# A kernel of attention and two MLPs: the second turn of the first MLP's results added in DRAM by the storing DMA

## The chip, the cores and the metric

The kernel runs on one core of a Trainium2 chip. The metric is the device time of one execution in microseconds; the median of several executions is compared. In the texts PE is TensorE (the matmul engine), PEld its loading of weights, DVE VectorE, ACT ScalarE, POOL GpSimd, and SP SyncE, which here issues nearly all DMAs. Each engine takes its own instructions in order; an instruction that reads what another engine writes waits for a semaphore.

## The reference, cut to what matters

```python
def reference(q, k, v, moe, moe2):                 # q, k, v: 4 x 8 heads x 576 x 64
    scores = (q @ k.transpose(0, 1, 3, 2)) / 8.0
    scores = where((rel >= 0) & (rel < 128), scores - slopes * abs(rel), -1e9)
    attn = softmax(scores) @ v
    x = attn.transpose(0, 2, 1, 3).reshape(2304, 512)
    h = x @ moe.w_in                               # 512 -> 2048
    x = (maximum(h, 0) + moe.alpha * minimum(h, 0)) @ moe.w_out
    h = maximum(maximum(x @ moe2.w1, x @ moe2.w2), x @ moe2.w3)   # 512 -> 768
    return h @ moe2.w_out                          # 2304 x 512
```

All of it is in fp32. `rel` is the distance of a key behind its query, so each token attends to itself and the 127 tokens before it.

## The kernel before, in words

The kernel has three stages that overlap: the attention, the first MLP and the second MLP. A matmul of fp32 numbers is done as three matmuls on rounded parts: each operand is split into a high part (an ACT cast, L521) and the rest (a subtraction on DVE or POOL, L523). Some weights are first put into another form of words by a chain of small steps on ACT, DVE and POOL (L501 to L514); these are the many `v<-v` and `wt<-wt` steps of a trace.

Attention: scores (L872), a pass over them on DVE (L903), exponentials on ACT (L909, L914), a scaling on POOL (L921), transposes by a matmul with the identity (L931), a copy of the transposed block out of PSUM on ACT (L939, into `w_d` early and into `pt` later), the values (L951, early L968 and L975), and copies of the result out of PSUM (L983 for the late groups, L998 and L1000 for the others).

First MLP: the 2304 tokens lie in nine blocks of 256, in five groups, `GROUPS = ((0, 1), (2, 3), (4,), (5, 6), (7, 8))`. For groups 0 to 2 a hidden step computes 128 hidden units (12 matmuls: L1034, L1035, L1036), DVE applies the activation (L1040, L1043), ACT and DVE split the result into `g` (L1013, L1014), and 12 products (L1062) add to the group's four PSUM banks `xb`. A step is of 512 columns for groups 0 and 1, and of 256 for group 2 and the first steps of group 0. `JOBS` sets the sequence: group 0 with hidden units 0 to 8 (its first turn), group 1 with all 16, group 0 with units 9 to 15 (its second turn), group 2. Groups 3 and 4 are computed by `pair_mlp`, with block products in fewer multiplications (L679, L713); group 4 in two turns, by halves of the hidden units.

Where a group has two turns (0 and 4), each turn's results are copied out of PSUM (L1077, or L727 in `drain`) and stored in a DRAM tile of its own, `x2d0_0` and `x2d0_1`, `x2d4_0` and `x2d4_1`. `sum_of_turns(k)` (L566) loads both in eight pieces of 128 KB, adds them on POOL (L563) and stores the sum in a third tile, from which the second MLP reads (`tokens`, L1087). The second MLP (`second_mlp`, L1082) has products L1225, L1250 and L1350 and starts when the pair MLP is done.

What sets the order: every piece of work is an `Op` of a `Plan` with its engine and dependencies, and the order in which all of them are issued, on all engines, is written out in a packed table, `ORDER`. `Plan.issue` (L137) goes through it, models the start of each op, and where the model sees a gap on PE between 12 and 130 us it puts matmuls that compute nothing into the next free bank (L461, `FILL_ONE` 0.215 us each in the model). L455 and L623 are single matmuls of the same kind that the table places. Pools of buffers set further waits: `o` and `ve` have two buffers, `wt` and `g` three, `hb` and `sb` two PSUM banks each, `xb` four banks that one group holds at a time.

## Time and profile before

| | us |
|---|---|
| median of 3 executions | 775.29 (775.09 to 775.59) |
| the profiled execution | 775.46 |
| its span, first to last instruction | 773.6 |
| PE busy | 758.2 (98%) |
| DVE busy | 577.5 (75%) |
| ACT busy | 447.3 (58%) |
| POOL busy | 283.9 (37%) |
| DMA queue of SP | 67.8% of 16 engines |

All durations that follow come from the profiled execution. Its granted PE clock is 1.00 in all stretches shown, of 2.4 GHz. A row of the timeline gives the start, the duration, the engine, the line, the operation and its tiles, and in square brackets how long the engine had been idle before and what released it. A busy time can hold overlapping instructions, since matmuls are pipelined: what one costs is read from start to start.

### The profile page before, as it was taken

To read this page: it belongs to the slowest core of one execution; us is meant where nothing else is said; L and a number is where in the kernel's file an instruction comes from. 1 tells how busy PE (TensorE), PEld (TensorE's weight loads), DVE (VectorE), ACT (ScalarE), POOL (GpSimd) and SP (SyncE) were. 2 spreads that over 40 slices of the span, in tenths; PEclk is the share of its full clock that TensorE was granted. 3 is DMA by queue.
4 is the path that set the end of the run, shared out by engine and by line. 5 is a ranking of instruction groups with operands and counts; after the bars stand their busy time and mean duration, and the time that the engine had idled before them with its cause. 6 is when DMAs were issued, how large, how long until landed. Compare 5 with 4: busy or idle time off the path is not lost.

```text
span 773.6 us, 17304 instructions
## 1 busy us (share of the span) xinstructions
PE 758.2 (98%) x6018; PEld 665.4 (86%) x6022; DVE 577.5 (75%) x1457; ACT 447.3 (58%) x1235; POOL 283.9 (37%) x385
## 2 busy tenths in 40 slices
...
GB/s 306 289 233 254 167 167 250 171 198 191 208 193 177 162 249 190 92 215 182 262 230 233 374 141 223 272 312 271 340 261 244 319 361 367 179 300 240 182 2 83
DMA packets 93096, 175.75 MB, mean 227 GB/s; under 512 B 11088, under 2 KB 53712, under 8 KB 93008
## 3 DMA queue, kind: packets, MB, share of 16 engines
q1 hardware_dynamic: 92544, 174.11, 67.8%
...
## 4 chain that ended last, share of the span: by engine, by line
PE 93%; ACT 3%; DMA 1%; DVE 1%; issue 0%; ACTq 0%; SPq 0%; DVEq 0%
PE xb L1062 15%; PE sb L1225 13%; PE hb L1225 13%; PE xb L713 6%; PE xb L1350 5%; PE hb L1034 5%; PE sb L679 5%; PE hb L679 5%; PE hb L1035 5%; PE hb L1036 5%; PE sb L951 3%; PE hb L713 3%; PE sb L713 3%; PE sb L931 3%; PE sb L872 2%; PE xb L1250 2%
## 5 line engine op out<-in xcount | busy, mean ns | idle before, releaser
L1062 PE MATMUL xb<-g,w_a 128*128 128x512 f32 (+1 forms) x624 | 125.3, 347 | 0.6 <-DVE z L903 0.6
L1062 PEld LDWEIGHTS xb<-g,w_a 128*128 128x128 f32 x624 | 97.5, 189 | 18.6 <-issue 5.8
L921 POOL TENSOR_SCALAR p<-p,z 128x192 f32<-128x192 f32 x144 | 74.1, 530 | 67.5 <-DVE z L917 63.0
L1034 PE MATMUL hb<-x_a,w_a 128*128 128x512 f32 (+1 forms) x208 | 73.5, 353 | 0.6 <-DVE x_a L1000 0.6
L909 ACT ACTIVATE p<-p,z 128x192 f32<-128x192 f32 x144 | 64.5, 452 | 12.2 <-DVE z L903 11.3
L1035 PE MATMUL hb<-x_a,w_a 128*128 128x512 f32 (+1 forms) x208 | 70.9, 341 | 0.0
L1036 PE MATMUL hb<-x_a,w_a 128*128 128x512 f32 (+1 forms) x208 | 70.8, 340 | 0.0
L514 POOL TENSOR_TENSOR v<-v,p 128x192 int32<-128x192 int32 (+1 forms) x72 | 41.6, 580 | 62.7 <-DVE v L511 21.8
L1225 PE MATMUL sb<-w_e,w_a 128*128 128x384 f32 x306 | 59.5, 335 | 0.0
L514 POOL TENSOR_TENSOR wt<-wt,w_b 128x512 int32<-128x512 int32 x32 | 42.9, 1344 | 30.5 <-issue 10.4
L1225 PEld LDWEIGHTS sb<-w_e,w_a 128*128 128x128 f32 x306 | 53.5, 188 | 0.2
L1013 ACT CAST g<-hb 128x512 fp32r<-128x512 f32 (+1 forms) x52 | 25.3, 486 | 42.0 <-DVE hb L1043 40.2
L523 DVE TENSOR_TENSOR w_a<-wt,w_a 128x512 fp32r<-128x512 f32 (+1 forms) x60 | 43.5, 728 | 7.4 <-ACT w_a L521 5.3
L521 ACT CAST w_a<-wt 128x512 fp32r<-128x512 f32 (+1 forms) x78 | 42.9, 563 | 9.5 <-DVE wt L563 4.0
L713 PE MATMUL xb<-g,w_a 128*128 128x512 f32 x192 | 46.8, 389 | 0.0
L1225 PE MATMUL hb<-w_e,w_a 128*128 128x384 f32 x234 | 46.4, 334 | 0.0
L1034 PEld LDWEIGHTS hb<-x_a,w_a 128*128 128x128 f32 x208 | 39.4, 189 | 7.2 <-issue 1.7
L1225 PE MATMUL hb<-w_e,x_a 128*128 128x384 f32 x234 | 45.2, 335 | 0.0
L1040 DVE TENSOR_SCALAR t<-hb,alpha_sb 128x512 f32<-128x512 f32 (+1 forms) x52 | 32.3, 621 | 15.9 <-PE hb L1036 15.4
L903 DVE CUSTOM_DVE_ANT_0 p<-sb,rel 128x192 f32<-128x192 f32 x112 | 35.3, 352 | 11.0 <-PE sb L872 4.9
L1036 PEld LDWEIGHTS hb<-x_a,w_a 128*128 128x128 f32 x208 | 39.4, 189 | 4.5
L1035 PEld LDWEIGHTS hb<-x_a,w_a 128*128 128x128 f32 x208 | 39.5, 190 | 3.7
...
## 6 DMA issues: line engine op xcount, KB each, us to landing
...
```

The source lines that it names most:

```text
L514: add("pool", 0.08 + n / 430, due - 5, lambda: nc.gpsimd.tensor_tensor(out=wt().bitcast(I32), in0=wt().bitcast(I32), in1=words(0), op=ALU. ...
L521: add("act", 0.05 + n / 1100, due, lambda: nc.scalar.copy(w()[:, 0, :n], of()), r=[of], w=[w])
L523: add("pool" if pool_lo else "dve", 0.08 + n / 430 if pool_lo else 0.07 + n / 960, due + 1, lambda: eng.tensor_tensor(out=w()[:, 1, :n], i ...
L679: nc.tensor.matmul(to(), w()[:, a, ws], xs[k]()[:, b], start=(first and at_m == 0), stop=(last and at_m == 5), skip_group_check=True)
L713: nc.tensor.matmul(bs[m](), W_out[f]()[:, a, cols], g[f]()[:, b], start=(opens and f == fs[0] and not a and not b), stop=(closes and f == ...
L909: exps.append(add("act", 0.45, due - 10 + a, lambda i=i, n=n, p=p: nc.scalar.activation(out=part_of_p(p, n), in_=part_of_p(p, n), func=AF. ...
L921: z.readers.append(add("pool", 0.4, at_a + 0.2, lambda i=i, n=n, p=p: nc.gpsimd.tensor_scalar(out=part_of_p(p, n), in0=part_of_p(p, n), sc ...
L1034: nc.tensor.matmul(to, wi()[:, 0, ws], x[:, 0, cols], start=(kk == 0), stop=False)
L1035: nc.tensor.matmul(to, wi()[:, 1, ws], x[:, 0, cols], start=False, stop=False)
L1036: nc.tensor.matmul(to, wi()[:, 0, ws], x[:, 1, cols], start=False, stop=(kk == KD - 1))
L1062: nc.tensor.matmul(to, wo()[:, a, ms], g()[:, b, :n], start=(opens and not a and not b), stop=(closes and ends), skip_group_check=apart)
L1225: nc.tensor.matmul(to()[:, :TILE], Qs[q]()[:, a, ws], x[:, b], start=(first and n == 0), stop=(last and n == 5), skip_group_check=True)
```

## The change

`sum_of_turns` goes, and with it 32 loads, 16 adds on POOL and 16 stores. Each group has one DRAM tile, `x2d0` to `x2d4`. A new helper, `stored`, issues the stores: those of a first or only turn as before from SP; those of the second turn of groups 0 and 4 from POOL, with `accum_op=ALU.add`, so that the DMA adds its data to what lies in DRAM. There are four such DMAs for each of the two groups, 256 KB each. In the plan they are still counted as SP's, at twice the cost of a plain store. `tokens` reads the group's one tile.

The table `ORDER` is another one altogether (one line of each stands below), and the model puts 29 fillers (L461 before, L458 after) instead of 17.

```diff
@@ -250,116 +250,113 @@
 ORDER = (
-    'c-'
...
+    'c-jrq0|FR2768B(JE?8kwr$(C-TvCPZQHhO+qSzqcNh!|5<p_0Pzn-3Nhl5-'
...
@@ -563,19 +560,13 @@
         add(eng, 0.08 + n / 430 if eng == "pool" else 0.07 + n / 960, due, lambda: e.tensor_tensor(
             out=to(), in0=one(), in1=two(), op=op), r=[one, two, *inplace], w=[to], port=True)
 
-    def sum_of_turns(k, due):
-
-        x2_d[k, 2] = dram.tile([P, KD, 2 * N], F32, name=f"x2d{k}_2")
-        x2_b[k, 2] = Buf(None, None, None)
-        for i in range(2 * KD):
-            kk, cols = i // 2, slice(i % 2 * N, (i % 2 + 1) * N)
-            u, w = (ve_r.new().part(lambda t: t.rearrange("p a b d -> p (a b d)")) for _ in range(2))
-            for one, turn in ((u, 0), (w, 1)):
-                add("sp", 0.5, due + 8 * i, lambda one=one, turn=turn, kk=kk, cols=cols: nc.sync.dma_start(
-                    out=one(), in_=x2_d[k, turn][:, kk, cols]), r=[x2_b[k, turn]], w=[one])
-            add_two("pool", N, due + 8 * i + 4, u, u, w, ALU.add)
-            add("sp", 0.5, due + 8 * i + 5, lambda u=u, kk=kk, cols=cols: nc.sync.dma_start(
-                out=x2_d[k, 2][:, kk, cols], in_=u()), r=[u], w=[x2_b[k, 2]])
+    def stored(due, cost, o, key, view, again, of=lambda t: t):
+
+        b = x2_b[key]
+        if again:
+            add("sp", 2 * cost, due, lambda: nc.gpsimd.dma_start(out=view(x2_d[key]), in_=of(o()), accum_op=ALU.add), r=[o, b], w=[b])
+        else:
+            add("sp", cost, due, lambda: nc.sync.dma_start(out=view(x2_d[key]), in_=of(o())), r=[o], w=[b])
 
     def words_ahead(due, until):
 
@@ -722,8 +713,7 @@
                 o = o_r.new() if m == 3 or key != (4, 1) else g_r.new().part(lambda t: t[:, 0].bitcast(F32))
                 copy, eng = ((nc.scalar.copy, "act"), (nc.vector.tensor_copy, "dve"))[m % 2]
                 add(eng, 0.62, due + six * m, lambda m=m, o=o, copy=copy: copy(o(), bs[m]()), r=[bs[m]], w=[o])
-                add("sp", 1.0, due + six * m + 1, lambda m=m, o=o: nc.sync.dma_start(
-                    out=x2_d[key][:, m, :], in_=o()), r=[o], w=[x2_b[key]])
+                stored(due + six * m + 1, 1.0, o, key[0], lambda t, m=m: t[:, m, :], key == (4, 1))
 
         whole = x_b.new()
         oA, now, s, E = [whole.part(lambda t, m=m: t[m]) for m in range(KD)], begin, 0, {}
@@ -800,7 +790,7 @@
             drain(oB, (4, half), now + six)
             now += 4 * six
             if not half:
-                stores = x2_b[4, 0].writers[-1:]
+                stores = x2_b[4].writers[-1:]
                 for f in range(8):
                     fetch_weights("in", f, IN_AT[f], now - 20 + 2 * f, stores if f > 3 else ())
                 for f in range(8):
@@ -1002,8 +992,7 @@
                 in1=part_of(x, 0, n).bitcast(F32), op=ALU.subtract), r=[psv[n]], w=[x], after=[hi])
 
 
-    x2_d = {(k, turn): dram.tile([P, KD, len(cs) * N], F32, name=f"x2d{k}_{turn}")
-            for k, cs in enumerate(GROUPS) for turn in range(2 if k in (0, 4) else 1)}
+    x2_d = {k: dram.tile([P, KD, len(cs) * N], F32, name=f"x2d{k}") for k, cs in enumerate(GROUPS)}
     x2_b = {key: Buf(None, None, None) for key in x2_d}
     st = {"turn": 0}
 
@@ -1075,8 +1064,7 @@
                 o = o_r.new()
             copy, eng = ((nc.scalar.copy, "act"), (nc.vector.tensor_copy, "dve"))[m % 2]
             add(eng, 0.12 + n / 1000, due, lambda m=m, o=o, copy=copy: copy(o()[:, :n], x2()[m][:, :n]), r=[x2], w=[o])
-            add("sp", n / 512, due, lambda m=m, o=o, turn=turn: nc.sync.dma_start(
-                out=x2_d[k, turn][:, m, :], in_=o()[:, :n]), r=[o], w=[x2_b[k, turn]])
+            stored(due, n / 512, o, k, lambda t, m=m: t[:, m, :], k == 0 and not turn, lambda t: t[:, :n])
 
 
     def second_mlp(begin):
@@ -1091,8 +1079,7 @@
                 g0, g1 = cs[0] * N, (cs[-1] + 1) * N
                 a, b = max(lo, g0), min(lo + TILE, g1)
                 if a < b:
-                    key = (k, 2 if k in (0, 4) else 0)
-                    yield x2_b[key], x2_d[key][:, kk, a - g0:b - g0], slice(out_at, out_at + b - a)
+                    yield x2_b[k], x2_d[k][:, kk, a - g0:b - g0], slice(out_at, out_at + b - a)
                     out_at += b - a
 
         def right_of(p, due):
@@ -1613,10 +1600,8 @@
             todo.append((i, hidden_of(i)))
             later(LATER)
     later(0)
-    sum_of_turns(0, at[-1])
     words_ahead(at[-1] + 60, at[-1] + 150)
     begin = pair_mlp(at[-1])
-    sum_of_turns(4, begin + 10)
     second_mlp(begin)
     plan.issue()
 
```

Lines of the new kernel lie about ten below those of the old: scores L862, transposes L921, copies of transposed blocks L929, values L941, copies of results L973, hidden steps L1023 to L1025, activation L1029 and L1032, splits L1002 and L1003, products L1051, copies out of the product banks L1066.

The end of the attention, on PE. Before, the scores of one pair of blocks (`sb_4464`, `sb_4467`) are followed by transposes, and products lie between these and the values (L951) of the next pair:

```order
L872 MATMUL sb_4464<-qkv_4288 64x192
L872 MATMUL sb_4467<-qkv_4288 64x192
L931 MATMUL sb_4519<-ident,p_4401 128x128 x3
L931 MATMUL sb_4523<-ident,p_4404 128x128 x3
L1062 MATMUL xb_4542<-g_4275,w_a 128x512 x2
L1062 MATMUL xb_4543<-g_4275,w_a 128x512 x2
L1062 MATMUL xb_4544<-g_4275,w_a 128x512 x2
L1062 MATMUL xb_4545<-g_4275,w_a 128x512 x2
L951 MATMUL sb_4561<-pt_4536,v_4301 64x64 x2
L951 MATMUL sb_4564<-pt_4536,v_4301 64x64 x2
```

After, a hidden step (its last rows are shown) lies ahead of the transposes, and the values that read the copy of what was transposed (`pt_4541` is copied from `sb_4528` and `sb_4532`) come next:

```order
L1024 MATMUL hb_4490<-x_a,w_a 128x512
L1025 MATMUL hb_4490<-x_a,w_a 128x512
L921 MATMUL sb_4528<-ident,p_4390 128x128 x3
L921 MATMUL sb_4532<-ident,p_4395 128x128 x3
L941 MATMUL sb_4551<-pt_4541,v_4320 64x64 x2
L941 MATMUL sb_4554<-pt_4541,v_4320 64x64 x2
L941 MATMUL sb_4551<-pt_4541,ve_4397 64x64 x2
```

The hidden step has moved between scores and transposes, and the products that stood between transposes and values have gone from there. The same pattern stands once more two pairs earlier (`sb_4310`, `pt_4325`, `sb_4331`). Behind the values of `sb_4551` and `sb_4554` the next transposes follow, into the bank that held them:

```order
L941 MATMUL sb_4554<-pt_4541,ve_4397 64x64 x2
L941 MATMUL sb_4551<-pt_4541,v_4320 64x64 x2
L941 MATMUL sb_4554<-pt_4541,v_4320 64x64 x2
L921 MATMUL sb_4583<-ident,p_4508 128x128 x3
L921 MATMUL sb_4587<-ident,p_4516 128x128 x3
L1051 MATMUL xb_4597<-g_4281,w_a 128x512 x2
```

Before, four products stand at this place. In the order of ACT the copies of `sb_4554` and `sb_4551` out of PSUM (L973) come right behind the copies into `pt_4541`.

The passage from group 0's second turn to group 2, on PE. Before, the last rows of a hidden step of group 2 and the first product of that group, which reads `g_4879`:

```order
L1036 MATMUL hb_4973<-x_a,w_a 128x256
L1034 MATMUL hb_4973<-x_a,w_a 128x256
L1035 MATMUL hb_4973<-x_a,w_a 128x256
L1036 MATMUL hb_4973<-x_a,w_a 128x256
L1062 MATMUL xb_4998<-g_4879,w_a 128x256 x2
L1062 MATMUL xb_4999<-g_4879,w_a 128x256 x2
L1062 MATMUL xb_5000<-g_4879,w_a 128x256 x2
L1062 MATMUL xb_5001<-g_4879,w_a 128x256 x2
```

After, the same place; the step shown, `hb_4940`, is the second of group 2, and the first is `hb_4917`, right before it and right behind the last products of group 0:

```order
L1025 MATMUL hb_4940<-x_a,w_a 128x256
L1023 MATMUL hb_4940<-x_a,w_a 128x256
L1024 MATMUL hb_4940<-x_a,w_a 128x256
L1025 MATMUL hb_4940<-x_a,w_a 128x256
L1051 MATMUL xb_4973<-g_4971,w_a 128x256 x2
L1051 MATMUL xb_4974<-g_4971,w_a 128x256 x2
L1051 MATMUL xb_4975<-g_4971,w_a 128x256 x2
L1051 MATMUL xb_4976<-g_4971,w_a 128x256 x2
```

The first product now reads `g_4971`, made from `hb_4917`, one hidden step earlier. On DVE `g_4879` was made five hidden steps and several products ahead of its reader:

```order
L1040 TENSOR_SCALAR t_4860<-hb_4825,alpha_sb 128x256
L508 TENSOR_SCALAR v_4847<-v_4847 128x192
L1043 SCALAR_TENSOR_TENSOR hb_4825<-hb_4825,t_4860 128x256
L511 SCALAR_TENSOR_TENSOR v_4847<-p_4812,v_4847 128x192
L1014 TENSOR_TENSOR g_4879<-hb_4825,g_4879 128x256
```

After, between the last product of group 0 and `g_4971`:

```order
L1066 COPY wt_4933<-xb_4600 128x512
L560 TENSOR_TENSOR wt_4938<-x_c 128x512
L1066 COPY o_4953<-xb_4598 128x512
L1029 TENSOR_SCALAR t_4962<-hb_4917,alpha_sb 128x256
L502 TENSOR_SCALAR v_4958<-v_4958 128x192
L1032 SCALAR_TENSOR_TENSOR hb_4917<-hb_4917,t_4962 128x256
L505 TENSOR_SCALAR v_4958<-v_4958 128x192
L502 TENSOR_SCALAR v_4958<-v_4958 128x128
L508 SCALAR_TENSOR_TENSOR v_4958<-p_4886,v_4958 128x192
L505 TENSOR_SCALAR v_4958<-v_4958 128x128
L1003 TENSOR_TENSOR g_4971<-hb_4917,g_4971 128x256
```

The two copies out of the product banks (L1066) and a difference for the pair MLP (L560) stand ahead of the activation of `hb_4917`, and small steps of a weight's conversion inside it.

POOL, behind group 0's second turn. Before, an add of the two turns (`ve`) stands among conversions (L514) and splits (L523):

```order
L563 TENSOR_TENSOR ve_5734<-ve_5734,ve_5770 128x256
L523 TENSOR_TENSOR w_a<-wt_5611,w_a 128x512
L514 TENSOR_TENSOR v_5764<-v_5764,p_5745 128x128
L514 TENSOR_TENSOR v_5832<-v_5832,p_5796 128x192
L514 TENSOR_TENSOR v_5832<-v_5832,p_5802 128x192
L523 TENSOR_TENSOR x_a<-wt_5855,x_a 128x512
L514 TENSOR_TENSOR v_5887<-v_5887,p_5834 128x128
```

After, the DMAs that add (`x2d_308` is `x2d0`) stand some 30 rows earlier in the queue, among the like:

```order
L567 DMA x2d_308<-o_4936 128x512
L511 TENSOR_TENSOR v_4958<-v_4958,p_4886 128x192
L511 TENSOR_TENSOR v_4958<-v_4958,p_4901 128x128
L520 TENSOR_TENSOR w_a<-x_c,w_a 128x512 x2
L511 TENSOR_TENSOR v_4989<-v_4989,p_4911 128x192
L567 DMA x2d_308<-o_4953 128x512
L511 TENSOR_TENSOR v_4989<-v_4989,p_4956 128x192
L567 DMA x2d_308<-wt_4931 128x512
L520 TENSOR_TENSOR w_a<-x_c,w_a 128x512
L511 TENSOR_TENSOR v_5065<-v_5065,p_5019 128x128
L520 TENSOR_TENSOR w_a<-x_c,w_a 128x512
L567 DMA x2d_308<-wt_4933 128x512
```

The adds are gone from POOL's queue, and four issues of DMAs are in it, of which `o_4936`, `o_4953`, `wt_4931` and `wt_4933` are the sources. The four of group 4 stand in POOL's queue in the same way, close to its end, ahead of its last splits.

## Rows read from the trace of the kernel before

**Rows 1.** The page, part 1: busy time, share of the span, instructions, by engine

```profile
PE 758.2 (98%) x6018; PEld 665.4 (86%) x6022; DVE 577.5 (75%) x1457; ACT 447.3 (58%) x1235; POOL 283.9 (37%) x385
```

**Rows 2.** The page, part 4: the chain that ended last, shares by engine

```profile
PE 93%; ACT 3%; DMA 1%; DVE 1%; issue 0%; ACTq 0%; SPq 0%; DVEq 0%
```

**Rows 3.** Stretches: length; busy time (instructions) by engine; PE clock, DMA share, GB/s

```profile
25.00:50.00 25.00, 23.04 (x294) 17.63 (x293) 22.79 (x77) 23.84 (x81) 15.23 (x22) 1.00 0.87 290
50.00:75.00 25.00, 24.13 (x373) 21.86 (x374) 23.39 (x87) 24.81 (x83) 12.91 (x20) 1.00 0.68 219
75.00:100.00 25.00, 25.00 (x306) 20.70 (x305) 22.98 (x70) 21.94 (x69) 14.13 (x18) 1.00 0.57 180
```

**Rows 4.** PE's waits: line waited <- releaser: total us, times, longest

```profile
PE sb L931 <- DVE z L903: 1.3, 1, 1.3
PE hb L623 <- DVE g L1014: 0.7, 1, 0.7
...
PE xb L1350 <- DVE ve L1264: 0.5, 1, 0.5
```

**Rows 5.** The adds of the turns: xcount, busy, mean ns, idle before, releaser; DMA issues

```profile
L563 POOL TENSOR_TENSOR ve<-ve,ve 128x256 f32<-128x256 f32 x16 | 13.0, 810 | 42.1 <-DMA ve<-x2d 42.1
...
ve<-x2d SPq DMA_DIRECT2D x32, 128.0 KB, 3.8
...
x2d<-ve SPq DMA_DIRECT2D x18, 128.0 KB, 3.6
...
x2d<-g SPq DMA_DIRECT2D x3, 256.0 KB, 5.0
```

**Rows 6.** Stretches as in rows 3, from the end of group 0 on

```profile
275.00:350.00 75.00, 74.25 (x509) 69.22 (x508) 67.47 (x163) 42.56 (x114) 34.02 (x43) 1.00 0.60 184
```

**Rows 7.** Timeline of PE, early attention: start, us, instruction [idle before <-releaser]

```profile
23.11 0.55 PE L931 MATMUL sb<-ident,p 128*128 128x128 f32 x3 [0.73 <-DVE x_a L1000]
...
31.05 0.37 PE L872 MATMUL xb<-w_c 64*64 64x192 f32 x1 [0.62 <-DVE z L903]
...
31.87 1.91 PE L461 MATMUL sb<-ident 128*128 128x512 bf16 x8
...
44.97 1.06 PE L968 MATMUL sb<-w_d,v 128*64 128x64 f32 x16 [0.24 <-ACT w_d L939]
...
52.60 0.39 PE L1034 MATMUL hb<-x_a,w_a 128*128 128x256 f32 x1 [0.59 <-DVE x_a L1000]
```

**Rows 8.** Timeline of PE, end of the attention

```profile
258.82 0.83 PE L872 MATMUL sb<-qkv 64*64 64x192 f32 x16
260.92 0.85 PE L931 MATMUL sb<-ident,p 128*128 128x128 f32 x6 [1.26 <-DVE z L903]
```

**Rows 9.** Timeline of ACT, end of the attention

```profile
255.53 0.84 ACT L939 COPY pt<-sb 128x384 f32<-128x384 f32 x2
...
259.75 0.62 ACT L983 COPY o<-sb 128x128 f32<-128x128 f32 x2 [3.28 <-PE sb L872]
```

**Rows 10.** Timeline of PE, two hidden steps of 12 matmuls: first and last

```profile
41.03 0.28 PE L1034 MATMUL hb<-x_a,w_a 128*128 128x256 f32 x1
...
43.79 0.28 PE L1036 MATMUL hb<-x_a,w_a 128*128 128x256 f32 x1
```

**Rows 11.** Timeline of DVE, behind the last products of group 0

```profile
292.06 0.69 DVE L1077 COPY wt<-xb 128x512 f32<-128x512 f32 x1 [0.21 <-PE xb L1062]
...
293.87 0.47 DVE L1040 TENSOR_SCALAR t<-hb,alpha_sb 128x256 f32<-128x256 f32 x1
294.26 1.77 DVE L563 TENSOR_TENSOR x_c<-x_c 128x512 f32<-128x512 f32 x1
...
296.13 0.42 DVE L1043 SCALAR_TENSOR_TENSOR hb<-hb,t 128x256 f32<-128x256 f32 x1
...
297.85 0.41 DVE L1014 TENSOR_TENSOR g<-hb,g 128x256 fp32r<-128x256 f32 x1
```

**Rows 12.** Timeline of PE, end of the hidden stage

```profile
334.07 0.38 PE L623 MATMUL hb<-ident 128*128 128x512 bf16 x1 [0.75 <-DVE g L1014]
```

More of the change, by code (lines that the diff above doesn't have):

```diff
@@ L361 @@
[L361 to L362 removed]
+    'c-jrq0|FR2768B(JE?8kwr$(C-TvCPZQHhO+qSzqcNh!|5<p_0Pzn-3Nhl5-'
+    'KmdVukQB;5N8q49LPFRGNx*@J2#^dkL;?#DAqtd*<PZ%aLur@`B_Jvo*aZP%KstyHsURjig$$4eVnKRH4Vj=EoPaD42Vz4;hzsoj'
+    'ATz{+eDDrBK{iMMSs^}Thm?>OHbD-k3i;s=REP4A6LLXCs0jt2E98bPP!RG!ZKwuYp%B!9yifz?!8WJ^nNd?{26dq`G=x4-'
+    '6skaBXap6YIrM`rPzf4CJ=hHWVFA>Kflv(kLK7$gCt){qhX&9Cx<M?o9a_L>_zx;WC)5%KKsU4(2E!mgFa)}zUa${#z!(?`3!x{p'
@@ new lines @@
+    'g5IzchQnAG2J>MAw1J)Q4BEm-'
+    '7zc}C5iEyMFdkmOb7&1OVF^ru{V)lp!b+F`r(qRLgI7=iO@~u38CJu4m<TiAHJpPza0V{GaI_3Q!fY6gR=^xM0Ey8|SPN(2AAEpM'
+    'Fb186S+EAy!D09e7vT!jL<eC#T!O!F8Lq+?0Q3fKKpb=j4#8L007oD;T8?hQH8=|Q;1;CA#~=&34hSVh$Kf_aL>S$LxF|A;gx<n^'
+    '$c_byf*t@vNl-jQ5J&M*Hbl`kcnl9gp{OV;lIRH}K-p16lpEzlr%?`+7iC0`AP-'
+    '80G|Gi4qwmlK8I%ttNBL1<WKlF!02M(AQFK%gWkNAf735GQ6cZIiiBN5n0snwPC=K$c7;1ulLM;?fTl@<;qX;M`o{3wcs;Cuejhd'
+    'shs12%ye#0W%7NtY!Q3_NY6-'
+    'OCRJJbTDL>*9jR1$SWB~UZm6_r9GP#u&Cl}0O257ZtX!hKLL)Dyi&{ZL<&8jV7|(P>;4{fBCxk!TU>j|QVMXaHJ?hM;n2EE<T?<H'
@@ new lines @@
+    'iUfj4E)$6;QpjW?o=7aDOd*m8C1Xo1lL{w|q|(bEBgph3rHCq{$%rzsOeG@8I5N42F5}7!VzNprV#w4YqnM(msZ=tJNGH~+$TEw_'
+    'B;v{GDv3-'
+    'gvx@a9n}{h>%gkb(N+Yw2Ybu9`FJs9WDw)hF63AKVrb;do%GoNHNGmhRJR+YcAU3EJGN+uQ(#ee~x5z8zskth>Oe9mv%rd{oA~VP'
+    '(s-Dgzv&#7@n=B~u$m}w=%qthDf-'
+    ';BPr1Ht7s)Ssq^2=K)qg<vIsV%C4yseh2#j3hop$f=dYO`9YR@y?cuq+~1*{$lJDk^uY>#CUCrf#UiYL(iq4yn~@hdQP9sGX{zE-'
+    '8!4y{d^msY=V!YM&}4E6OsmzC5DJ%6qD^EGN&X{i=#Qst%}2s*!FckEu$su`Vxb$m8m=I;*P6n(~A?r>e;-'
+    's)4K}8_M&lg={Ws%loR4Y$xl;tE#2Epz6v8s<FJN?x?P^m8>V5$o8_ee4?7lhw83sBRj}Ps-t|ZI?1Q1zV0i#$-'
@@ new lines @@
+    '(lmYM`H~w(_ldqn@iCva{?dyUQ-'
+    '}i|Qwv>t6Cd*<TKkz2ytlR}Ync)G#?(zEcC_a5+$x(=XKsIY{=AU)5*zN{y70<a_l&&60mr3;j(klpj?~JxYF8|I{ZnM*dLa<ajw'
+    '&{#2kR$X{xroGg+4t)|G?a*kXiSIWh5sw8@@#Cn>XC#TE#a)wlz>Lqf4WO}JAub0UPdX?mQgIq3~>X}mO)v}oudWVdpBkKLq=rvO'
+    '671HXMdadlQ*GZ?>%L+P%j-{9B$ojbSI-'
+    '!oOqv)VF%1ttnj;eRcUGjk3EC=Y_a*I49qv@?Ou^y=7=z}t@PNMh7Z8Ex!r%%X}GPOP|<LkZhoIE1;$?fu#OrVqMe)^g`Ei>sf`a'
+    'hjapO?vXMSVtQ))(YanL?kH*X2r`R$r7^^i6q5rqs9OU3ppFmg)2{c}1quH)K}*RHoN=WCndzX47wFM*T(JllNtI{XjmHkK{A?Tt'
@@ new lines @@
+    '1dL^b7e?zLT%yd-'
+    '*|rm9OO!`Az23ALV!XM}Cq&<Y)Ot=F&eUQ@^BDx%FT9PyUvmkcy(P%A<+m>i=bxQ%dF4UTH;DP)5a35mZ!FKu1*3RCE<dB~~$1Oq'
+    'EZ^Qjt|$m0HD9g>-xsTP08lRT7n1B~nRMeqBr_Q^{2dl~UzWX;fjIR;5$Lb$XRSWl<SbE1gPZRV8#Gl}%+=nN$&-'
+    'Tjfx#bzW6c=Tv!ADV0wZ)%jH^T|iY-'
+    'g;fz%RJGN`RB=^Wmrw;&8Qn&=(=}CTRZ^8vWmP4W%(U0#RAp6OmDN>L1yxmb)zwr7U0u~u$xTOHM-'
+    '|j{RSHvEb<*8*Dzi%0Q{8oa)mhh2gY;_ML#H%dbWdGL57Ft&U|mi3($)1S-CH+MLv<CM-lR6e^h7;c*VKLVay?wv(35p#JxQ<7we'
+    '%QWTaVDQbX7f8kJNSaI6YI>)wA^!JzlTVbM#a_L2uF1^mIK}uhBE~JiS%V*Gu$Ty+E(mi}gaiL2uN1^)|g-@76nXHM3JM)qC_Vy-'
```

185 lines of the change are left out of this document (76 added, 109 removed).

## The prediction

> **What bounds the kernel now.** I read first the table of busy time by engine [rows 1]: TensorE (PE) is busy 758.2 of 773.6 us, 98%, the next engine, VectorE (DVE), 577.5. Then the chain of waits that ended last [rows 2]: 93% of it is PE's own work. So the time is PE's work plus the few microseconds in which PE has none, and an edit counts only if it changes one of these two. Where PE has none is read from the busy time by stretches [rows 3]: 23.04 and 24.13 of 25 us in the two slices from 25 to 75 us, and 25.00 behind them. In these two slices ScalarE (ACT) is busy 23.84 and 24.81 and DVE 22.79 and 23.39: the attention there is bounded by ACT and DVE, and PE follows. Last, the table of PE's waits [rows 4] names who ends each: DVE or ACT every time (the rows shown are those that places (b) and (d) below and the second MLP come back to), never GpSimd (POOL), never a DMA.
>
> **What is removed.** For each of two groups: eight times two loads of 128 KB, an add on POOL, a store of 128 KB [rows 5]. That is 16 adds of 0.81 us, 13.0 us of POOL, with 42.1 us in which POOL waits for the loads; 32 loads and 16 stores, 6.3 MB of transfers, out of the 175.75 MB of the whole kernel by the page. POOL is busy 37% of the span, and no wait of PE is ended by it or by a DMA. So what is removed has other work around it on every side: 0 us on the path. A gain by it is excluded by [rows 4]; it could come only by way of the order.
>
> **What is added.** Eight DMAs of 256 KB, issued by POOL, that add to what lies in DRAM. No DMA of the kernel before is issued by POOL, and none adds: the price is not in the trace. From below it is 0, since nothing that PE waits for is behind them. From above: the slowest plain store of this size (x2d<-g) takes 5.0 us from issue to landing [rows 5]; if POOL stood still for as long, the four of the first group would hold it 20 us. They stand among the splits of weights for the pair MLP, in which POOL is busy 34.02 of 75 us [rows 6], so 41 us are free. Each of the splits is needed some 9 us or more of PE's work later. I take 0, and up to +4 us if most of the 20 us falls ahead of the first split that PE needs. The readers of these sums are the second MLP's loads, tens of microseconds later; the next groups' loads stand behind them on SyncE (SP) and have the same slack.
>
> The Trainium skill, page "DMA: Bandwidth & Descriptors", section "Anatomy of one DMA — SWDGE (gpsimd) path", gives about 2.0 us plus bytes / 436e3 for such a DMA: as an estimate 2.6 us each, 10 us for a group. By it the term stays 0, since 10 us is less than the free time. No run here shows it yet.
>
> **What is moved: everything, by the new table.** PE has the same matmuls in both orders, DVE and ACT the same instructions. Four places differ in what PE can wait for.
>
> (a) The early attention. The plan fills PE's modelled gaps with matmuls that compute nothing (L461): 17 before, 29 now, 11 ahead of the first hidden step, 10 ahead of the next transposes, 5 and 3 at two later places. Eight of them take 1.91 us [rows 7], 0.24 each, so the added 12 are 2.9 us of PE. They cost that only if PE would have had work. Between 20 and 53 us PE waits eight times, 3.45 us together (0.73 and 0.15 ahead of the first hidden step, 0.62 and 0.22 around the next transposes, 0.59, 0.24, 0.31 and 0.59 later; five rows of this stretch, the first and the last wait among them, are [rows 7]). Ahead of the first hidden step 4 more fillers (0.96) take the place of 0.88 us of waits: +0.1. At the next place the number is the same. Later 8 fillers (1.9) stand where 1.18 us of DVE waits stood, in part elsewhere; I count half of these as covered: 1.9 - 0.6 = +1.3. Sum +1.4, and between -0.6 (all 3.45 us gone) and +2.9 (none gone).
>
> (b) The end of the attention, some 235 to 266 us. Before, scores (16 matmuls) are followed at once by transposes, and PE waits 1.26 us for DVE [rows 8]. Now 12 hidden matmuls of 512 columns lie between, about twice the 1.44 us that 12 of 256 take (place (c)), and cover it: -1.26. But at two places the values (L951) now come right behind the transposes whose ACT copy they read, with nothing between, and at a third the transposes come right behind values whose bank ACT must first copy out. The pair of copies ahead of the values takes 0.84 us, the pair behind the values 0.62 [rows 9]; with 0.15 to 0.3 us from PE to ACT and back, PE waits about 0.8, 0.9 and 0.6. From below, the nearest row is an early one, where values, at 44.97, stand right behind transposes and wait 0.24 [rows 7]: three times 0.24 is 0.7. From above 0.84 + 0.3 at the first two and 0.9 at the third (the chain of the softmax may end last there): 3.2. I take 2.3, as the late copies are the ones concerned. Net +1.0.
>
> (c) From group 0's second turn to group 2. Before, the hidden steps of group 2 lie between the last products of group 0, and the first product of group 2 reads a hidden result that was ready long before. Now all products of group 0 come first, then two hidden steps of 256 columns, then the product that reads the first of them. A step of 12 such matmuls takes 1.44 us, as 24 take 2.88 from the first start to the last [rows 10], so PE has 2.88 us to give DVE. In that time DVE does: two copies out of the product banks and a difference between, 1.81 us from start to start, as from 292.06 to 293.87 [rows 11]; then L1040 (0.47), one small step, L1043 (0.42), four small steps of a weight's conversion, which lie in the same way before L1014 at 297.85, 1.72 us behind L1043's start; I take 1.3, as one step less lies between; L1014 itself 0.41. With some 0.17 us until DVE sees the last product: 0.17 + 1.81 + 0.57 + 1.3 + 0.41 = 4.3, and 0.15 back to PE: 4.4 to 4.5. PE waits 4.45 - 2.88 = 1.6. From below 1.0, if the small steps stretch over 0.7 only; from above 2.8, since a difference like the one in this place, at 294.26, took 1.77 where the copy at 292.06 took 0.69 [rows 11]. +1.6.
>
> (d) The end of the hidden stage. The filler at 334.07 waits 0.75 for a subtraction on DVE [rows 12]; now four rounds of 12 products of 256 columns (5.8 us by the step of place (c)) lie in front of it. -0.75. What is late next is the pair MLP's first blocks, which wait for nothing in either trace now.
>
> The second MLP keeps its distances between product and reader in both orders; its waits of about 0.5 us [rows 4] stay, give or take 1 us.
>
> **Sum.** 1.4 + 1.0 + 1.6 - 0.75 = +3.25 on PE's path, 0 for the sums and the new DMAs. The profiled execution took 775.46 us, 0.17 above the median of the runs, 775.29; with 1.9 us of it outside the span of 773.6, which stay. 775.46 + 3.25 - 0.17 = 778.5. About 0.2%, 1.55 us, is what a measurement of this kernel can tell from no change.
>
> **Rivals.**
> No change: the fillers stand where PE would wait anyway (a is 0), and values behind transposes wait as little as in the early stage (0.7 at b). 0 + 0.7 - 1.26 + 1.6 - 0.75 = +0.3: 775.6. For it: ACT is busy 24.81 of 25 us at 50 to 75 us, so PE's early work may be worth nothing; against it: the 0.24 belongs to a value that needs one copy, not two. Chance 0.25.
>
> Faster: one mechanism, the early attention's feed. If the new order hands ACT and DVE their work so that all eight early waits go and the added fillers only stand in gaps that are there anyway, (a) is -3.45; with (b) to (d) as above -1.6: 773.7. It decides as soon as more of the true matmuls are done by 75 us than before. For it: the waits are real and the order was made afresh; against it: ACT has only 1.35 us free in those 50 us, so its work there cannot be done much sooner. Chance 0.17.
>
> POOL held: the new DMAs keep POOL so long that a split comes late, and PE waits at the first blocks of the pair MLP: +4, 782.5. It decides if a DMA holds POOL over some 5 us. For it: POOL writes them in a stretch in which DVE is hardly ever idle, 67.47 of 75 us [rows 6]; against it: 41 us of POOL are free. Chance 0.07.
>
> The Trainium skill speaks for this last one: "SBUF — State Buffer", section "Who interferes with whom", says that a DMA issued by GpSimd can be held while VectorE has the ports they share. By it the term of the added DMAs would be up to the +4 us and not 0; the trace has no such DMA, so neither agrees nor disagrees.
>
> The forecast itself, slower by 1.6 to 6 us: 0.51.
>
> **How the numbers follow.** Slower 0.51 + 0.07 = 0.58, within 0.2% 0.25, faster 0.17. The terms' bounds give: a -0.6 to 2.9, b -0.6 to 1.9, c 1.0 to 2.8, d -0.75, second MLP -1 to +1; all at the lower ends -1.9 (773.4), all at the upper +7.9 (783.2). Both at once are unlikely; 773.8 to 782.5 leaves out part of the faster case and of the case with POOL held, under 2 in 10.
>
> **What the changed profile would show.** PE's filler group with 29 instructions, and fewer or smaller waits before 53 us (a); PE's waits for the copies L939 at 235 to 266 us, two or three of 0.6 to 1.0, and none of 1.26 for DVE (b); one wait of PE for L1014 of 1.0 to 2.8 near 290 us (c); no wait at the filler behind the hidden stage (d); no add of x2d on POOL, POOL's DMAs with 256 KB, and no wait of PE that POOL or a DMA ends. The prediction is wrong if PE's waits of (b) and (c) are not there, or if PE waits at the beginning of the pair MLP.

## The result

The changed kernel takes 781.67 us (median of 4 runs, 781.52 to 782.55) against 775.44 for the kernel before on the same chip: 1.0078 times as long, with a 95% interval of 1.0063 to 1.0093. So it is slower, by 6.2 us. The profiled execution of after has a span of 779.9 us, 6.3 more than before.

Busy time by engine, the part of the page that answers [rows 1]:

```profile
PE 760.9 (98%) x6026; PEld 667.7 (86%) x6034; DVE 572.2 (73%) x1457; ACT 447.5 (57%) x1235; POOL 275.6 (35%) x377
```

PE is busy 2.7 us longer and idle 3.6 us longer (span minus busy time: 15.4 before, 19.0 after). POOL is busy 8.3 us less: its 16 adds of 13.0 us are gone, and eight issues of DMAs have come in. DVE has the same 1457 instructions and is busy 5.3 us less in them. Neither shortens the time. PE's waits, which answer [rows 4], without the one at the start (5.1 us, 4.8 before); columns as there:

```profile
PE sb L1212 <- ACT hb L1228: 3.2, 1, 3.2
PE xb L1051 <- ACT g L1002: 1.5, 1, 1.5
PE sb L941 <- ACT pt L929: 1.2, 2, 0.9
...
PE xb L1337 <- DVE ve L1251: 0.7, 2, 0.5
```

The largest of these has no counterpart before: 3.2 us at L1212, among the first products of the second MLP, which the pair MLP's last group still overlaps. The timeline of PE at this place, and the stretches around it (columns as in [rows 3]):

```profile
502.82 1.70 PE L1212 MATMUL sb<-w_e,w_a 128*128 128x384 f32 x6 [3.17 <-ACT hb L1228]
504.32 2.12 PE L1212 MATMUL hb<-w_e,w_a 128*128 128x384 f32 x6
506.24 1.55 PE L1212 MATMUL sb<-w_e,w_a 128*128 128x384 f32 x6
507.63 1.21 PE L1212 MATMUL hb<-w_e,x_a 128*128 128x384 f32 x6
508.68 1.55 PE L704 MATMUL hb<-w_a 128*128 128x512 f32 x6
```

```profile
500.00:505.00 5.00, 2.18 (x9) 2.17 (x10) 0.69 (x1) 1.41 (x4) 1.72 (x2) 0.85 0.44 100
505.00:510.00 5.00, 5.00 (x23) 4.78 (x22) 2.78 (x5) 2.14 (x5) 0.00 (x0) 0.80 0.95 234
510.00:515.00 5.00, 5.00 (x30) 4.95 (x30) 2.60 (x6) 1.87 (x4) 0.00 (x0) 1.00 0.57 166
```

Two things are to be seen. PE stands for 3.17 us, and behind that the granted clock is 0.85 and 0.80, which means that part of these 10 us ran at the lower level, 1.2 GHz; from 510 us on it is 1.00 (2.4 GHz). The groups of six matmuls start 1.50, 1.92 and 1.39 us apart (502.82, 504.32, 506.24, 507.63), where the last of them takes 1.05: three times 1.05 taken from the 4.81 leaves some 1.7 us more. So the place costs about 4.9 us, most of the loss.

Who made PE wait is read from the chain of waits in this stretch (start, us, what):

```profile
493.15 0.60 ACT g L715
494.03 7.37 DMA x2d<-g
501.52 0.70 DVE g L715
502.82 1.70 PE sb L1212 x6
```

and from DVE's own row:

```profile
501.52 0.69 DVE L715 COPY g<-hb 128x512 f32<-128x512 f32 x1 [6.01 <-DMA x2d<-g]
```

L715 is `drain`, which copies group 4's second turn out of PSUM. ACT made the first copy, into a buffer of `g`; POOL issued the adding DMA from it at 494.03; DVE's copy of the next bank was given **the same buffer** and had to wait until the DMA had landed, 7.37 us. Behind DVE's copy stands ACT's L1228, which writes a bank `hb` next, and behind that PE. The table of PE's waits names only the last of these, ACT; the DMA stands three steps behind it. Before, the three copies into `g` were placed in three buffers, and plain stores took them away.

### The profile page after: what moved, and what is told of

The parts are those of the page before. It is cut to its first block, busy times and chain, and to the rows that moved or that the text cites. A ratio compares the mean times of both kernels' runs of the same rounds, so it can differ in the third digit from the quotient of the medians.

```text
span 779.9 us, 17283 instructions
## 1 busy us (share of the span) xinstructions
PE 760.9 (98%) x6026; PEld 667.7 (86%) x6034; DVE 572.2 (73%) x1457; ACT 447.5 (57%) x1235; POOL 275.6 (35%) x377
## 4 chain that ended last, share of the span: by engine, by line
PE 92%; ACT 4%; DMA 2%; DVE 1%; issue 0%; ACTq 0%; DVEq 0%
PE xb L1051 15%; PE sb L1212 13%; PE hb L1212 13%; PE xb L1337 5%; PE xb L704 5%; PE sb L670 5%; PE hb L670 5%; PE hb L1023 5%; PE hb L1024 5%; PE hb L1025 5%; PE sb L941 3%; PE hb L704 3%; PE sb L704 3%; PE sb L862 2%; PE sb L921 2%; PE xb L1237 2%
## 5 line engine op out<-in xcount | busy, mean ns | idle before, releaser
L1051 PE MATMUL xb<-g,w_a 128*128 128x512 f32 (+1 forms) x624 | 123.7, 347 | 1.5 <-ACT g L1002 1.5
L1051 PEld LDWEIGHTS xb<-g,w_a 128*128 128x128 f32 x624 | 97.5, 190 | 18.4 <-issue 4.1
L1023 PE MATMUL hb<-x_a,w_a 128*128 128x512 f32 (+1 forms) x208 | 73.9, 355 | 0.0
L1025 PE MATMUL hb<-x_a,w_a 128*128 128x512 f32 (+1 forms) x208 | 70.9, 341 | 0.0
L1212 PE MATMUL sb<-w_e,w_a 128*128 128x384 f32 x306 | 60.5, 338 | 3.2 <-ACT hb L1228 3.2
L1212 PEld LDWEIGHTS sb<-w_e,w_a 128*128 128x128 f32 x306 | 54.1, 190 | 3.9 <-ACT hb L1228 3.6
L520 DVE TENSOR_TENSOR w_a<-wt,w_a 128x512 fp32r<-128x512 f32 (+1 forms) x60 | 45.6, 764 | 10.7 <-ACT w_a L518 10.6
L1212 PE MATMUL hb<-w_e,w_a 128*128 128x384 f32 x234 | 46.3, 339 | 0.0
L1023 PEld LDWEIGHTS hb<-x_a,w_a 128*128 128x128 f32 x208 | 39.4, 190 | 7.1 <-issue 2.2
L1212 PE MATMUL hb<-w_e,x_a 128*128 128x384 f32 x234 | 44.9, 334 | 0.0
L1002 ACT CAST g<-hb 128x512 fp32r<-128x512 f32 (+1 forms) x52 | 25.3, 487 | 33.3 <-DVE hb L1032 31.5
L1025 PEld LDWEIGHTS hb<-x_a,w_a 128*128 128x128 f32 x208 | 39.4, 189 | 4.5
L704 PEld LDWEIGHTS xb<-g,w_a 128*128 128x128 f32 x192 | 36.1, 188 | 7.5
```

The source lines that it names most:

```text
L520: add("pool" if pool_lo else "dve", 0.08 + n / 430 if pool_lo else 0.07 + n / 960, due + 1, lambda: eng.tensor_tensor(out=w()[:, 1, :n], i ...
L704: nc.tensor.matmul(bs[m](), W_out[f]()[:, a, cols], g[f]()[:, b], start=(opens and f == fs[0] and not a and not b), stop=(closes and f == ...
L1023: nc.tensor.matmul(to, wi()[:, 0, ws], x[:, 0, cols], start=(kk == 0), stop=False)
L1025: nc.tensor.matmul(to, wi()[:, 0, ws], x[:, 1, cols], start=False, stop=(kk == KD - 1))
L1051: nc.tensor.matmul(to, wo()[:, a, ms], g()[:, b, :n], start=(opens and not a and not b), stop=(closes and ends), skip_group_check=apart)
L1212: nc.tensor.matmul(to()[:, :TILE], Qs[q]()[:, a, ws], x[:, b], start=(first and n == 0), stop=(last and n == 5), skip_group_check=True)
```

## The experiments

All ratios are against the kernel before on the same chip; its median differs by up to 0.7 us from one comparison to another (775.44 to 776.11), so two runs are compared by their distances from it. Line numbers move a little from kernel to kernel, and the tiles tell which row is meant. The order table is edited by moving single rows of it; `op` numbers are those of the plan.

**1. Another slot for group 4's first adding DMA.** If that DMA is put behind the second one in POOL's queue, the copies get different buffers. Every engine but POOL keeps its order.

```diff
+        order.remove(2847)
+        order.insert(order.index(2849) + 1, 2847)
```

> The changed kernel with two of the DMAs that add, the first and the second of group 4, changed about in POOL's queue; every other instruction stands as in the changed kernel. By this the second drained bank is copied into a buffer of its own, where it was copied into the one that the first of these DMAs still reads. Theory 1, the held buffer: the wait of 3.17 us at 502.8 us and the low clock behind it (granted 0.85 and 0.80 in 500 to 510 us) go, 4 to 5 us: 776.7 to 777.7. Theory 2, the wait belongs to the order of the steps on DVE and ACT and would end on something else there: less than 1 us, 780.7 to 781.7.

777.42 us against 775.96, 1.0017 [1.0007, 1.0026]. The wait at L1212 is gone and the clock stays up. DVE's copy now waits for a product and for no DMA:

```profile
497.08 0.69 DVE L718 COPY g<-hb 128x512 f32<-128x512 f32 x1 [1.33 <-PE xb L707]
```

The same stretches:

```profile
500.00:505.00 5.00, 5.00 (x29) 4.84 (x28) 2.26 (x4) 3.17 (x6) 0.86 (x1) 1.00 1.07 167
505.00:510.00 5.00, 5.00 (x30) 4.87 (x29) 3.12 (x7) 1.87 (x4) 0.00 (x0) 1.00 0.97 302
```

This kernel is 1.5 us above the kernel before, where after is 6.2 above it. So the held buffer, with the clock that it cost, is worth some 4.8 us, which agrees with the 4.9 read from the trace.

**2. The same DMAs without the addition.** POOL still issues the eight stores; only `accum_op` is left out.

```diff
-... in_=of(o()), accum_op=ALU.add), ...
+... in_=of(o())), ...
```

> The changed kernel with the second turn's eight DMAs of 256 KB issued by POOL at the same places into the same tiles, as plain stores that do not add (the sums are left out: the second turn overwrites the first). Theory 1a, the adding makes the DMA slow to land: the landing falls from 5.4 us in the median and 7.4 at the place that PE waits for to the 3 to 5 us of the plain stores of the kernel before, and 2 to 4.5 us are won: 777 to 779.7. Theory 1b, what is slow is a DMA of POOL's own, whatever it does: landing and time stay, 781 to 782.

779.15 us against 775.96, 1.0040 [1.0025, 1.0055]. The wait at L1212 is 2.1 instead of 3.2 us, DVE's in front of it 4.5 instead of 6.0, and the clock is 1.00 from 500 to 515 us. The time is 3.0 us less than after's (3.2 above before instead of 6.2), about the 1.1 of the wait and the 1.7 of the clock. What the addition itself costs is seen from all rows of the line, first after, then this kernel (issue on POOL in ns, minimum, median, maximum; and the landing):

```profile
L567 POOL DMA_DIRECT2D x2d<-g x3: 857/858/868, 494.0 to 503.6; - x3
...
DMA to landing us min/median/max: 4.1/5.4/7.9
```

```profile
L567 POOL DMA_DIRECT2D x2d<-g x3: 539/542/559, 493.6 to 502.0; - x3
...
DMA to landing us min/median/max: 2.6/3.3/6.3
```

An adding DMA lands some 2 us later than a plain one from the same queue and holds POOL 0.3 us longer. The shared buffer does the rest: the second copy still goes into the first one's buffer, and without the addition the wait is still there.

**3. Plain stores from SP, in the new order.** This leaves out both additions and takes POOL out of it; what remains is the new order of PE, ACT and DVE.

```diff
-... nc.gpsimd.dma_start(out=view(x2_d[key]), in_=of(o()), accum_op=ALU.add), ...
+... nc.sync.dma_start(out=view(x2_d[key]), in_=of(o())), ...
```

> Left out: both additions (the second turn overwrites the first). The changed kernel, its order untouched, with the eight adding DMAs of POOL issued as plain stores from SP. It separates what the new order costs by itself from what the DMAs cost. Theory 'the source of an adding DMA is held': a plain store of this size from SP lands in 2.8 to 4.2 us where the adding one took 7.37, so the second copy into the shared buffer waits 1.5 to 3 us instead of 6.0, PE's wait at the drain of group 4 falls from 3.2 to under 1 us and the clock there stays at 1.00; what is left is the order's own: 777.4 as a_other_slot, between 776.6 and 778.2, with PE's wait for the first products of group 2 at 1.3 to 2.0. Rival 'the order alone makes the wait, the buffer would be late with any store': the wait stays at 2 us or more, 779 to 781. Rival 'the order by itself costs nothing, all of the loss is the DMAs': 775.4.

777.36 us against 776.11, 1.0014 [1.0005, 1.0023]. No wait at L1212; DVE's copy waits for a product and for no DMA. But the copies have three buffers again in this kernel, as before, so what was expected of a plain store from the shared buffer could not come about; run 2 is the one that shows a plain store there, from POOL's queue.

```profile
497.03 0.69 DVE L715 COPY g<-hb 128x512 f32<-128x512 f32 x1 [1.50 <-PE xb L704]
```

PE's waits are otherwise those of after:

```profile
PE xb L1051 <- ACT g L1002: 1.5, 1, 1.5
PE sb L941 <- ACT pt L929: 1.2, 2, 0.9
```

So the loss parts in two: the new order costs 1.3 us by itself, the DMAs in it, with the buffers that go with them, the other 5.

**4. The change in the order of before.** `ORDER` of before is kept, the sums' rows are dropped and the new stores stand where the old ones stood; PE, DVE and ACT have the rows of before.

```diff
+        sums = [(1858, 1890), (2886, 2918)]
...
+            if any(a <= i < b for a, b in sums):
+                continue
```

> The change without the new order: each group's second turn is added in DRAM by POOL's DMAs, the 64 steps of the sums are gone, and all other steps follow the table of the kernel before; the orders on PE, DVE and ACT are those of before. If the DMAs that add cost nothing by themselves and the 6.2 us are the new order's (with the buffer that it shares), the time is that of the kernel before, 775.4, within 0.8. If the DMAs that add cost something wherever they stand, through POOL's or the transfers' time, it is 777 or more. If the removed loads, adds and stores were worth something, 774.5 or less.

778.42 us against 775.96, 1.0035 [1.0021, 1.0049]: slower, though PE, DVE and ACT keep their order. PE waits three times where group 2 begins, 3.3 us in all, in an execution of 780.51, the longest of the five; the two longest waits are shown. In front of them stand four adding DMAs in a row on POOL:

```profile
302.48 1.22 PE L1065 MATMUL xb<-g,w_a 128*128 128x256 f32 x8 [1.36 <-ACT g L1016]
307.19 1.22 PE L1065 MATMUL xb<-g,w_a 128*128 128x256 f32 x8 [1.57 <-ACT g L1016]
```

```profile
295.89 1.97 POOL L581 DMA_DIRECT2D x2d<-o  x2
297.19 2.45 POOL L581 DMA_DIRECT2D x2d<-wt  x2
298.30 1.97 POOL L525 TENSOR_TENSOR v<-v,p 128x192 int32<-128x192 int32 x1
```

The chain runs from POOL's conversion at 298.30 over a load of weights, which needs the buffer that it frees, to ACT's conversion of that load, to the split of `g`, to PE. The load is late, and it is also slow:

```profile
300.30 5.97 DMA p<-in_w
```

In the kernel before, the two loads of this kind and size from 297 to 310 us took 2.9 us in the median. So this is in part a version of the rival "POOL held", at another place than I had looked; which part is POOL's and which the transfers' this run does not tell.

**5. The four DMAs spread among the conversions.** As 4, one DMA behind every second instruction of POOL, those from `wt` first.

```diff
+        order.insert(first, 1745)
+        for one, ops in ((1747, 2), (1741, 4), (1743, 6)):
```

> As c_old_order, but group 0's four DMAs that add no longer stand in a row in POOL's queue: two steps of POOL lie between each and the next, and the two from the wt buffers come first. In c_old_order they stood in a row, took 0.86 to 1.9 us of POOL each, and the conversion steps behind them were late; ACT then waited for a load that waited for these, and PE three times for ACT, 3.3 us in all at 302 to 310 us. Theory: it is the row of four that cost this; with steps between them POOL catches up, these waits of PE fall to 0.5 us or less, and the time is 775.4 to 776.6. Rival: POOL's time for them is spent wherever they stand among these conversions, and the time stays at 777.5 or more.

777.29 us against 775.83, 1.0023 [1.0013, 1.0034]: better than 4 by the median, though the intervals overlap, and still slower than before; it lies between the two times expected. One wait of PE of 1.27 us is left, at 307.47. ACT's conversions stand in front of it, and they wait for loads; first this kernel, then the kernel before:

```profile
303.93 0.38 ACT L525 ACTIVATE v<-p 128x192 f32<-128x192 f32 x1 [1.76 <-DMA p<-in_w]
...
306.52 0.38 ACT L525 ACTIVATE v<-p 128x192 f32<-128x192 f32 x1 [0.85 <-DMA p<-in_w]
```

```profile
302.36 0.38 ACT L501 ACTIVATE v<-p 128x192 f32<-128x192 f32 x1 [0.32 <-DMA p<-in_w]
...
304.88 0.38 ACT L501 ACTIVATE v<-p 128x192 f32<-128x192 f32 x1
```

The load that ends at 306.4 was issued at 301.30 and took 5.14 us; the one of before was issued at 301.12 and was there when ACT wanted it at 304.88. So the issue is 0.2 us later here, and the landing 1.5 or more. From 297 to 310 us the adding DMAs fill more of the 16 DMA engines than all other transfers, which would explain the slow load but does not by itself prove it:

```profile
q0 software_dynamic: 555, 1.01, 56.8%
q1 hardware_dynamic: 1008, 1.28, 32.4%
```

**6. The same, with three of the DMAs where POOL has nothing to do.** They stand behind the conversion at 303.7 us instead.

```diff
-        for one, ops in ((1747, 2), (1741, 4), (1743, 6)):
+        for one, ops in ((1743, 6), (1741, 6), (1747, 6)):
```

> All sums are computed. c_spread with three of group 0's four adding DMAs moved behind the conversion of a weight on POOL that stood at 303.7 us there, into a stretch in which POOL of before has nothing to do for 3.0 us (303.6 to 306.7); the first one stays at 295, where POOL of before waits 1.75 us. The instructions of PE, DVE, ACT and SP stand in the same rows as in c_spread. Theory 'POOL's time': the conversions run as early as in before, no wait of PE near 307 us, 775.8 with bounds 775.2 and 776.3, no slower than before: the change as such is then worth 0. Rival 'the adding DMAs' traffic or their hold on VectorE delays the conversions wherever they stand': the wait stays at 1 us or more, 777 or above.

780.77 us against 775.82, 1.0062 [1.0048, 1.0075]: the time is the rival's, the mechanism is neither's. POOL's conversions do run as early as in before, as the last one ahead of the three DMAs shows, first this kernel, then the kernel before:

```profile
303.00 0.61 POOL L538 TENSOR_TENSOR v<-v,p 128x192 int32<-128x192 int32 x1 [0.30 <-DVE v L535]
```

```profile
303.02 0.61 POOL L514 TENSOR_TENSOR v<-v,p 128x192 int32<-128x192 int32 x1 [0.29 <-DVE v L511]
```

So POOL's time, which I had blamed, is not what costs here; it is a buffer again. SP's waits from 300 to 312 us, and the chain:

```profile
SPq L680 <- DMA x2d<-wt: 6.7, 1, 6.7
```

```profile
303.54 4.60 DMA x2d<-wt
308.15 0.33 SPq L680
308.60 4.31 DMA p<-in_w
```

L680 loads into the `wt` buffer from which the adding DMA reads. SP waits 6.7 us for it, in order, and behind it in its queue stands the load of the next weights (`p`), for which ACT's conversions and in the end PE wait (1.27 us at 314.80 and 2.20 at 320.13).

**7. Group 0's second turn stored plainly.** As 4, but group 0's four DMAs are plain stores from SP, and its addition is left out; group 4's still add.

```diff
+        if again and key == 0:
+            add("sp", 2 * cost, due, lambda: nc.sync.dma_start(out=view(x2_d[key]), in_=of(o())), r=[o, b], w=[b])
```

> Left out: the addition for group 0 (its second turn overwrites the first). The change with the order of before; the four second-turn stores of group 0 are plain ones from SP again, those of group 4 are still adding DMAs from POOL. Theory 'POOL's time for the four DMAs delays the conversions of the weights': POOL's queue at 295 to 303 us is that of before again, so the wait of PE for the first products of group 2 near 303 to 307 us (1.27 us in c_spread, 3.3 in c_old_order) is gone and the time is that of before, 775.5, between 775.0 and 776.2. Rival 'something else of the change costs, for instance that the loads and stores of the sums are gone from SP's queue and other transfers start sooner': the wait of 1.3 us or more stays, 777.3 as c_spread. If taking the sums out is itself worth something, below 775.0.

776.28 us against 775.82, 1.0006 [0.9997, 1.0015]: no difference from before that could be told (-0.2 to +1.2 us), and no wait at group 2. So the adding DMAs of group 0 were the cost of 4 and 5. Group 4's DMAs and the sums that are gone come to nothing together; that each does is not shown by the time, but the trace has PE busy 30.00 of the 30 us from 490 to 520, as before, so group 4's drain makes no wait in that order.

**8. Fewer fillers.** In the changed kernel the model puts 21 instead of 29.

```diff
-FILL_FROM, FILL_TO, FILL_LESS, FILL_ONE = 12.0, 130.0, 0.3, 0.215
+FILL_FROM, FILL_TO, FILL_LESS, FILL_ONE = 12.0, 36.0, 0.3, 0.215
```

> The changed kernel without the last 8 of its 29 fillers (5 ahead of one hidden step, 3 ahead of one transpose, some 1.9 us of PE). If these stand in time in which PE would work, as the prediction counted for 1.3 us, the time falls by 1 to 1.9 us: 779.8 to 780.7. If PE would wait there for ACT and DVE in any case, it stays at 781.7 within 0.4, and the eight reappear as waits before 53 us.

781.83 us against 775.96, 1.0076 [1.0059, 1.0092], as after. In the profiled execution, the shortest of the four (780.72), PE is busy 1.0 us less from 25 to 75 us (24.04 and 24.42 of 25, after 24.50 and 24.94), and waits have come back in its place (0.70 at 42.64, 0.47 at 53.40). Its wait at L1212 is 2.5 us, with the clock at 1.00.

**9 and 10. Mending (c) and (b), both on top of 1.** In a_boundary the small conversion steps and the difference between the product banks' copies and `g_4971` are moved behind it on DVE; in a_both products of group 0 are besides set between transposes and values again.

```diff
+        for op, behind in [(2847, 2849), (2409, 1730), (1981, 2409), (1982, 1981), (1988, 1982), (1983, 1988), (1989, 1983)]:
```

> As a_other_slot, and on DVE one difference for the pair MLP and five small conversion steps, which stood ahead of or inside the activation of group 2's first hidden step, now stand right behind it. If place (c) is what the prediction said, DVE's work ahead of the first product of group 2, its wait of 1.5 to 2.0 us goes: 775.4 to 776.2. If the wait goes and comes back further on, since the same conversions are then late for POOL and ACT, the time stays at 777.4 within 0.5.

> As a_boundary, and at the end of the attention the products of group 0's second turn are set between transposes and values again, as in the kernel before: place (b). The waits of PE for ACT's copies there, 0.95 and 0.48 of the 1.67 us, should go: 1.0 to 1.4 us below a_boundary, 774.0 to 775.2, and so below both kernels if all of (b), (c) and the held buffer were what the change cost. If instead the products then wait for their banks, which the results of group 1 still hold, it stays at a_boundary's time within 0.4.

778.20 us (1.0032 [1.0020, 1.0045]) and 778.68 us (1.0041 [1.0026, 1.0056]) against 775.83: nothing gained over run 1's 1.0017. PE's waits, of a_boundary and of a_both:

```profile
PE xb L1054 <- ACT g L1005: 0.8, 2, 0.4
...
PE hb L1026 <- DVE g L1006: 0.8, 1, 0.8
```

```profile
PE xb L1054 <- ACT g L1005: 3.4, 3, 2.6
```

In the first the wait of (c), 1.95 us in run 1, parts into three smaller ones of 1.6 together; in the second only 0.24 of (b)'s 1.67 is left, but the products that cover them are missing in front of (c), where the three waits for ACT are 3.4. By this the waits of (b) and (c) share one stock of ready products: what covers the one uncovers the other. No version of the change came out faster than before.

## Point by point

**The bound.** Right: PE's work and its gaps. Every version's time follows PE's waits, and that POOL is busy 8.3 us less and DVE 5.3 is not found in the time.

**What is removed: 0.** Right as far as run 7 can tell, within -0.2 to +1.2 us and together with group 4's DMAs.

**What is added: 0, up to +4.** This step failed: in the order as it stands the DMAs cost 5.0 us by run 3, of which run 1 puts 4.8 on one held buffer. I priced an adding DMA by the time that its issue takes from POOL, and asked who reads what it writes. I did not ask who wants **the buffer that it reads from**. The bound from above was too low as well: the 5.0 us of [rows 5] is the median of three plain stores and not the slowest, the slowest store of the drain before took 6.8, and an adding DMA up to 7.9. That a wait of PE can cost clock as well, here 1.7 us, stood in no term. The rival "POOL held" had nearly the size (+4) and not the mechanism: POOL is held 0.86 to 1.05 us per DMA in after, not 5, and PE waits for no split. A row of the trace before had shown the pattern: DVE's copy of the same `drain` waits for a plain store.

```profile
501.37 0.69 DVE L724 COPY o<-hb 128x512 f32<-128x512 f32 x1 [2.75 <-DMA x2d<-o]
```

It cost nothing there, since PE did not need that bank yet; but it says that in this drain a copy waits for a store to land, and that a store that lands later moves it.

The Trainium skill, page "DMA: Bandwidth & Descriptors", section "Anatomy of one DMA — SWDGE (gpsimd) path", gives about 2.0 us plus bytes / 436e3, by which I had estimated 2.6 us per DMA. The fastest plain store from POOL took 2.6, the median 3.3; the adding ones took 5.4, up to 7.9. For an addition in DRAM the measurement decides, and the estimate is short by half. Of the rule of the Trainium skill, page "SBUF — State Buffer", section "Who interferes with whom", that a DMA issued by GpSimd can be held while VectorE has the ports they share, the trace shows little: the three from `g`, at whose issue DVE is mostly idle, took 0.86 to 0.87 us on POOL, those of group 0, among DVE's work, 0.87 to 1.05.

**(a) The early attention: +1.4.** Too high. Three waits of 1.12 us are left of eight of 3.45 [rows 7], at 20.10, 22.09 and 49.21 (0.16, 0.78, 0.18); the recorded fillers take 6.60 us instead of 4.10. So +2.5 - 2.3 = +0.2; some fillers have no record (25 of 29 have one, 15 of 17 before), and with the 0.24 of the prediction for each of the twelve it is +2.9 - 2.3 = +0.6. Either is near the case that I had under "no change". Run 8 says the same from the other side. PE's stretches, which answer [rows 3]:

```profile
25.00:50.00 25.00, 24.50 (x326) 18.93 (x328) 22.75 (x80) 24.55 (x80) 16.50 (x21) 1.00 0.85 293
50.00:75.00 25.00, 24.94 (x354) 22.50 (x349) 24.25 (x84) 24.16 (x80) 13.19 (x20) 1.00 0.67 217
```

**(b) The end of the attention: +1.0.** The waits stand at the three places named, in size below what I took:

```profile
246.17 0.66 PE L941 MATMUL sb<-pt,v 64*64 64x64 f32 x5 [0.24 <-ACT pt L929]
...
260.54 0.34 PE L941 MATMUL sb<-pt,v 64*64 64x64 f32 x8 [0.95 <-ACT pt L929]
...
261.95 0.85 PE L921 MATMUL sb<-ident,p 128*128 128x128 f32 x6 [0.48 <-ACT o L973]
```

0.24 + 0.95 + 0.48 - 1.26 = +0.4. The wait for DVE [rows 8] is gone as forecast.

**(c) Into group 2: +1.6.** It was 1.49 (1.95 in run 1, in the same order), and the steps of DVE come as counted, but for one:

```profile
291.92 0.42 DVE L1032 SCALAR_TENSOR_TENSOR hb<-hb,t 128x256 f32<-128x256 f32 x1
```

```profile
292.79 1.70 PE L1051 MATMUL xb<-g,w_a 128*128 128x256 f32 x12 [1.49 <-ACT g L1002]
```

One thing in it was wrong without changing the sum: the first product waits for ACT's cast (292.37, behind L1032), not for DVE's split, which is later still (293.11). And one small step between, L502, took 1.32 us, for which my sum had 0.1. The two errors cancel: DVE came later to L1032, and PE did not need what DVE does behind it.

**(d) The end of the hidden stage: -0.75.** Right; no wait stands there [rows 12].

**The second MLP: 0, give or take 1.** It was +1.4: seven waits of 2.6 us after 650 us, three of 1.2 before. They are there in run 3 too, so the order makes them, not the DMAs.

**The sum.** For the order alone I had +3.25; run 3 measures +1.3. The terms as measured give 0.2 + 0.4 + 1.5 - 0.75 + 1.4 = 2.75, and its profiled span is 2.0 longer than before's. Some 0.7 of these 2.0 may not be the change's, as the kernel before took 776.11 beside run 3 and 775.44 in the result. The rest of the difference lies in PE's busy time, which is only 1.3 us longer in run 3 than before, where the fillers alone add 2.5; I have not traced it. The 781.7 came out above my 778.5, near the upper end of the range, because the DMAs cost 5 us and not 0, and no further above because the order cost 2 us less than I had: (a) and (b) were too high by 1.8, the second MLP too low by 1.4, and the rest is what I have not traced. These misses go against each other. So the path (PE and its gaps), the direction, and the places (a) to (d) were right; that the time lies within the range, with its largest wait at a place that the prediction did not name, is in part luck.
